# Sink attention and an erf-softplus feed-forward layer: another order of the vector engine's early work and of the early loads

## The chip, the cores and the metric

The kernel runs on one core of a Trainium2 chip. The metric is the device time of one execution in microseconds (us); lower is better. A core has a tensor engine (PE; PEld is its loading of stationary operands), a vector engine (DVE), a scalar engine (ACT), a GpSimd engine (POOL), and a sync engine (SP), which here issues nearly all transfers. Each engine has a queue of instructions that is fixed when the kernel is built.

## The reference

Attention over 4 batches, 8 heads, 768 positions and a head size of 64, with a causal window of 128 positions and 4 "sink" positions that every row sees; its output, as 3072 rows of 512, goes through a feed-forward layer with the gate `h * erf(softplus(h))`. All weights are given in 8-byte floating point.

```python
scores = q @ k.T / sqrt(D)
keep = (pos[None, :] < n_sink) | ((rel >= 0) & (rel < window))
a = softmax(where(keep, scores, -1e9))
x = concat_heads(a @ v)                 # 3072 x 512
h = x @ w_in                            # 512 x 2048
g = h * erf(log1p(exp(h)))
out = g @ w_out                         # 2048 x 512
```

## The kernel before

**Attention.** The rows are worked in 12 groups of 256. A group has four *steps*, one for each pair of heads, so there are steps 0 to 47; steps 0 to 3 are group 0, 4 to 7 group 1, 8 to 11 group 2. A step goes through `prep` (transposes of q and k on PE, copy to `kq` on ACT), `score` (products `ps` on PE; two masked copies L358 and four fused row maxima L363 on DVE, the *maxima* of the step below; four exponentials L367 on ACT), `norm` (sum and reciprocal L374/L375 on DVE, then four multiplications, L380 on ACT for steps 2 to 7; the sink columns `snk` L386 on DVE), `ptrans` (transposes `tp`, `ts` on PE, copies `pa`, `pz` on ACT, selections on POOL), `av` (products on PE) and `xfin` (copies L466 or L471/L472 into the input of the feed-forward layer).

**Feed-forward.** A group has 16 tiles of 128 hidden units. Two of them share one PSUM tile `h`; there are two such tiles in turn, so the pair after next can start only when DVE has read the earlier one. ACT makes `r` and three `u` from a tile (L658 to L663), DVE three products `gf` from them (L667), of which the first also reads `h`. The projection `o` (L687) of a pair needs its third `gf`. Group 0 multiplies in plain f32 with blocks `wf` (L641); from group 1 on `h` uses split blocks `wt` and inputs `xh`, `xl` in three products (L645).

**Weights.** The 32 blocks of 128x512 (16 of `w_in`, 16 of `w_out`) are loaded as 512 KB of 8-byte numbers (`ws`, L531) and turned into f32 blocks `wf` on DVE by three integer instructions each (L543, L548, L551; *conversion* below), in the order of their use (number `wn`). The conversion of block `wn` waits for that of `wn - 2`.

**Order.** Every helper is called with a priority, and a scheduler decides from these, and from its own model of the times, in which order each engine's queue is written. On the chip an engine then takes its queue in that order. `follow(prev, ins)` forces `ins` behind `prev` on an engine and costs no semaphore; `mark` keeps instructions for it: `("t", s)` the last maximum of step s, `("s", s)` its sink columns, `("c", wn)` the end of a conversion, `("p", s)` the last transpose. Eight transfers are in flight at most: each waits for the landing of the one eight places before it.

Of the kernel before, what the change touches and what calls it, by code (L numbers as in the profile page):

```python
# [19 lines left out]
P = 128  # L20
# [20 lines left out]

NM, NA = 2, 8

PW, EA = 256, 12
# [8 lines left out]
def kernel(  # L53
# [77 lines left out]
    def fast_path():  # L131
        with ExitStack() as st:
# [65 lines left out]
            def load(s, what="qk"):  # L198
                g, c = divmod(s, NPAIR)
                b, gb = divmod(g, GPB)  # L200
                d = stp.setdefault(s, {})
                for nm, src in zip("qkv", (q, k, v)):
                    if nm not in what:
                        continue
                    n0 = 1 if nm == "v" else 0
                    t = d[nm] = raw.tile([P, 2 + n0, 2, D], F32, tag=nm, bufs=1 + AL if nm == "v" else 1, name=f"{nm}_{s}")
                    m0 = 0 if gb == 0 else n0
                    for h in range(2):
                        nc.sync.dma_start(
                            t[:, n0 - m0 :, h, :],  # L210
                            src[b, 2 * c + h, gb * GT - m0 * P : (gb + 1) * GT, :].rearrange("(n p) d -> p n d", p=P),
                        )
                if gb == 0 and "v" in what:
                    for z in range(2):
                        for i in range(2):
                            for h in range(2):
                                r0, e = HP * (1 - z) + 2 * SW * i + SW * h, 2 * c + h
                                nc.sync.dma_start(vz[r0 : r0 + SW, z, i, e], v[b, e, :SW, :])
# [92 lines left out]
            def score(s, prev):  # L311
# [37 lines left out]
                for hf, x, y in ((lo, X[0], X[0] + KB), (hi, X[0] + 64, X[0] - 80)):  # L349
                    for t in (both,) if both is not None else ps:  # L350
                        t = t if both is not None else t.rearrange("p (h t) -> p h t", h=1)
                        n = t.shape[1]
                        o, w = (
                            t[hf, :, z : z + 2 * dx].rearrange("p h (i t) -> p h i t", i=2)[:, :, i0:, e : e + 64]
                            for z, e in ((min(x, 64), x - min(x, 64)), (min(y, 64), y - min(y, 64)))
                        )
                        mk = tri[hf].rearrange("p (a b t) -> p a b t", a=1, b=1).broadcast_to([64, n, 2 - i0, 64])
                        nc.vector.copy_predicated(o, mk, w)  # L358
                for i in range(2):
# [11 lines left out]
            def norm(s):  # L371
# [4 lines left out]
                for i in range(2):  # L376
                    for h in range(2):
                        p = pst[:, s % RING, i, h, :P]
                        if NM <= s < NA:
                            nc.scalar.mul(p, p, sm[:, i, h : h + 1])  # L380
                        else:
                            nc.vector.tensor_scalar_mul(p, p, sm[:, i, h : h + 1])
# [8 lines left out]
            def ptrans(s):  # L391
# [4 lines left out]
                for i in range(2):  # L396
                    for h in range(2):
                        mark["p", s] = nc.tensor.transpose(out=tp[:, h, i, :], in_=pst[:, s % RING, i, h, :P], identity=ident)
                nc.tensor.transpose(out=ts, in_=d["snk"], identity=ident)
                pa = d["pa"] = work.tile([P, 2, 2, P], F32, tag="pa", bufs=AL, name=f"pa_{s}")  # L400
# [5 lines left out]
                for hf in (lo, hi):  # L406
                    other = hi if hf == lo else lo
                    y = ts[hf, other].rearrange("p (a b t) -> p a b t", a=1, b=1)
                    nc.scalar.copy(pz[hf, :, :, other], y.broadcast_to([HP, 2, 2, HP]))
                if i0:  # L410
# [97 lines left out]
            def attn(a):  # L508

                for what, fn, s in sorted(plan.get(a, ()), key=lambda x: (STAGES.index(x[0]), x[2])):  # L510
                    with at(a, what):
                        fn(s)
# [11 lines left out]
            def wload(n):  # L524
# [3 lines left out]
                if src.dtype == F32:  # L528
                    nc.sync.dma_start(t[:, :DM].bitcast(F32), src)
                else:  # L530
                    nc.sync.dma_start(t, src.bitcast(I32))  # L531

            def wconv(n, wn):
# [11 lines left out]
                )  # L545
                follow(mark["s", 2] if wn < 1 else mark["t", 3] if wn < 3 else mark["s", 3], first)
                follow(mark.get(("c", wn - 2)), first)
# [39 lines left out]
            for m in range(-LEAD, NG * NF + LAG + 2):  # L587
# [20 lines left out]
                if live:  # L608
                    if f == 0:
                        with at(a, "hid"):  # L610
                            mlp.hidden(hp, xp[g], f)
                    if f % 2 == 1:
                        with at(a, "act"):
                            gs[m // 2] = mlp.act(hp, m, g < 2)

                while wn < 32 and a >= 1 and (wn < (0, 0, 3, 5)[a - 1] if a < 5 else wn < 2 * a - 4 or need(order[wn]) <= m + W1):
                    with at(a, "wc"):
# [10 lines left out]
    class make_mlp:  # L628
# [6 lines left out]

        def hidden(self, hp, xt, f):
            j, fs = f // 4, slice(f % 4 * P, f % 4 * P + P)
            o = hp[:, f % 2, :]
            if len(xt) == 1:
                for c in range(NC):  # L640
                    nc.tensor.matmul(o, wf[NC * j + c][:, fs], xt[0][:, c, :], start=(c == 0), stop=(c == NC - 1))  # L641
                return
# [202 lines left out]
```

## Time and profile before

| | us |
|---|---|
| median of 3 runs | 738.61 (738.1 to 738.76) |
| the profiled execution's own time | 738.85 |
| its span in the trace | 737.1 |
| PE busy | 715.7 (97%) |
| ACT busy | 552.3 (75%) |
| DVE busy | 485.2 (66%) |
| POOL busy | 210.3 (29%) |

Shares are means over the whole span. The change concerns the first 105 us, in which the engines are loaded otherwise than in the rest: there the transfers of the weights, the conversions on DVE and the start of the feed-forward layer lie on top of each other. "Idle before" in a row is the time for which the engine stood still ahead of an instruction, with what ended it.

### The profile page before, as it was taken

The page shows a single profiled execution, that of the slowest core. Times are in us where ns is not written, and L with a number is a line of the kernel's source. Part 1 is how long each engine was busy: PE and PEld are TensorE (multiplying, and loading weights), DVE is VectorE, ACT ScalarE, POOL GpSimd, SP SyncE. Part 2 cuts the span into 40 slices and gives each one's busy share as a digit, 9 for nine tenths or more (in the row PEclk, how much of TensorE's full clock was granted, in tenths as well). Part 3 has the DMA queues.
Part 4 walks back from the last instruction along what each step waited for, and adds up shares of the span by engine and source line. Part 5 has one row for each costly group of instructions (what it writes and reads, how often), then busy time and mean ns, then how long its engine had stood idle before and what let it go on. Part 6 is the DMA issues. An engine that isn't in the chain of part 4 may idle for free. (4 is left out here: it accounts for less than half of the span.)

```text
span 737.1 us, 16408 instructions
## 1 busy us (share of the span) xinstructions
PE 715.7 (97%) x5808; PEld 595.4 (81%) x5808; DVE 485.2 (66%) x1367; ACT 552.3 (75%) x1313; POOL 210.3 (29%) x302
## 2 busy tenths in 40 slices
PE   6789999999999999999999999999999999999997
PEld 3656667766888888888888888888898888898885
DVE  7999997676755665665656666665665566475252
ACT  4687759986877876976975975976886886677572
POOL 3411232111323322332333232233224223233221
PEclk9999999999999999999999999999999999999999
DMA  7999111121222222212212211311321221200000
GB/s 174 278 335 380 31 37 55 31 56 38 76 58 52 51 53 49 65 43 57 67 39 56 76 38 44 83 36 40 78 49 37 79 55 38 67 13 2 29 1 34
DMA packets 113001, 53.07 MB, mean 72 GB/s; under 512 B 91728, under 2 KB 105552, under 8 KB 112912
## 3 DMA queue, kind: packets, MB, share of 16 engines
q1 hardware_dynamic: 112352, 51.87, 26.3%
q8 instruction: 49, 0.80, 0.5%
q14 instruction: 40, 0.33, 0.2%
q10 hardware_dynamic: 560, 0.07, 0.1%
HBM read 38.01 MB, written 6.29 MB: 60 GB/s over the span
## 5 line engine op out<-in xcount | busy, mean ns | idle before, releaser
L645 PE MATMUL h<-xh,wt 128*128 128x256 f32 x1408 | 277.6, 285 | 0.2 <-DVE u L667 0.2
L645 PEld LDWEIGHTS h<-xh,wt 128*128 128x128 f32 x1408 | 223.9, 188 | 7.7 <-issue 1.7
L675 POOL TENSOR_TENSOR g<-u,g 128x512 fp32r<-128x512 f32 x80 | 106.2, 1328 | 341.6 <-DVE g L674 341.0
L645 PE MATMUL h<-xl,wt 128*128 128x256 f32 x704 | 197.9, 282 | 0.0
L663 ACT ACTIVATE u<-r 128x512 f32<-128x512 f32 x288 | 161.7, 622 | 12.6 <-DVE gf L667 4.7
L645 PEld LDWEIGHTS h<-xl,wt 128*128 128x128 f32 x704 | 132.2, 188 | 4.9 <-issue 1.2
L667 DVE SCALAR_TENSOR_TENSOR u<-u,u 128x512 f32<-128x512 f32 x160 | 124.6, 779 | 16.2 <-ACT u L663 1.6
L691 PE MATMUL o<-wt,g 128*128 128x512 f32 x320 | 127.4, 398 | 0.0
L690 PE MATMUL o<-wt,g 128*128 128x512 f32 x320 | 127.3, 398 | 0.0
L692 PE MATMUL o<-wt,g 128*128 128x512 f32 x320 | 123.7, 398 | 0.2 <-POOLq L813 0.2
L667 DVE SCALAR_TENSOR_TENSOR u<-u,h 128x512 f32<-128x512 f32 x80 | 54.9, 687 | 85.8 <-ACT u L663 81.7
L416 POOL TENSOR_SCALAR_AFFINE_SELECT pz<-pa 64x256 f32<-64x256 f32 (+1 forms) x96 | 54.8, 571 | 151.8 <-ACT pa L405 148.5
L367 ACT ACTIVATE pst<-pst,neg 128x144 f32<-128x144 f32 x192 | 77.4, 406 | 27.0 <-DVE neg L363 26.0
L658 ACT ACTIVATE r<-h 128x512 f32<-128x512 f32 x96 | 56.6, 590 | 18.8 <-PE h L645 15.3
L690 PEld LDWEIGHTS o<-wt,g 128*128 128x128 f32 x320 | 60.0, 187 | 11.5 <-ACT ot L696 0.4
L692 PEld LDWEIGHTS o<-wt,g 128*128 128x128 f32 x320 | 59.0, 187 | 12.6 <-POOLq L813 0.7
L691 PEld LDWEIGHTS o<-wt,g 128*128 128x128 f32 x320 | 60.0, 188 | 10.5
L674 DVE CAST g<-u 128x512 fp32r<-128x512 f32 x80 | 34.6, 433 | 45.6 <-PE o L692 42.4
L659 ACT ACTIVATE r<-r 128x512 f32<-128x512 f32 x96 | 60.7, 632 | 2.5
L660 ACT ACTIVATE r<-r 128x512 f32<-128x512 f32 x96 | 60.6, 631 | 2.6
L687 PE MATMUL o<-wf,gf 128*128 128x512 f32 x128 | 58.4, 594 | 1.2 <-DVE gf L667 1.2
L297 ACT COPY kq<-tqk 128x512 f32<-128x512 f32 x48 | 27.8, 581 | 32.5 <-PE tqk L294 30.2
(88 smaller groups left out, 937.3 us busy)
## 6 DMA issues: line engine op xcount, KB each, us to landing
ws<-in_moe_w_in_dram SPq DMA_DIRECT2D x16, 512.0 KB, 6.3
ws<-in_moe_w_out_dram SPq DMA_DIRECT2D x16, 512.0 KB, 8.4
out_dram<-ot SPq DMA_DIRECT2D x24, 256.0 KB, 2.1
v<-in_v_dram SPq DMA_DIRECT2D x56, 96.0 KB, 2.2
q<-in_q_dram SPq DMA_DIRECT2D x80, 64.0 KB, 2.2
k<-in_k_dram SPq DMA_DIRECT2D x80, 64.0 KB, 2.1
vz<-v SPq DMA_DIRECT2D x80, 64.0 KB, 2.0
kq<-kq SPq DMA_DIRECT2D x28, 64.0 KB, 2.0
```

The source lines that it names most:

```text
L367: nc.scalar.activation(y, y, AF.Exp, bias=d["neg"][:, i, h : h + 1], scale=-1.0, accum_out=d["sum"][:, i, h : h + 1])
L645: last = nc.tensor.matmul(o, wt[NC * j + c][:, p, fs], xt[e][:, c, :], start=(m == 0), stop=(m == len(ops) - 1))
L658: nc.scalar.activation(r, h, AF.Tanh, bias=b_t, scale=0.5)
L659: nc.scalar.activation(r, r, AF.Square, bias=b_v, scale=-0.5)
L660: nc.scalar.activation(r, r, AF.Square, bias=b_r)
L663: sq = nc.scalar.activation(u, r, AF.Square, bias=b_a[i], scale=CS)
L667: pr = nc.vector.scalar_tensor_tensor(out=acc, in0=u, scalar=CC[i] * CS**2, in1=x, op0=ALU.add, op1=ALU.mult)
L675: nc.gpsimd.tensor_tensor(gl, acc, gh.bitcast(F32), op=ALU.subtract)
L687: nc.tensor.matmul(o, gt[0][:, ws], wf[16 + f], start=(f == 0), stop=(f == NF - 1))
L690: behind(nc.tensor.matmul(o, gh[:, ws], wt[16 + f][:, 0, :], start=(f == 0), stop=False))
L691: nc.tensor.matmul(o, gh[:, ws], wt[16 + f][:, 1, :], start=False, stop=False)
L692: nc.tensor.matmul(o, gl[:, ws], wt[16 + f][:, 0, :], start=False, stop=(f == NF - 1))
```

## The change

1. The conversion of block 0 follows the maxima of step 1 (before: the sink columns of step 2), may be scheduled from the first pass on, and the maxima of step 2 are put behind it.
2. The loads of q, k and v of group 2 are put behind the last weight load on SP.
3. The first instruction of the conversions 8, 10, 13 and 17 gets a fixed place: behind the maxima of step 4, the sink columns of step 4, the maxima of step 5, the sink columns of step 5.
4. Four smaller rules: the maxima of step 3 follow the sink columns of step 1; the multiplications of step 3 follow the `pz` copy of step 2; the first feed-forward product follows the `ts` transpose of step 2; `norm` of step 3 is called later in its pass.

No instruction is added or removed; places in the queues change.

```diff
+TURN = {8: ("t", 4), 10: ("s", 4), 13: ("t", 5), 17: ("s", 5)}
...
-                        nc.sync.dma_start(
-                            t[:, n0 - m0 :, h, :],
-                            src[b, 2 * c + h, gb * GT - m0 * P : (gb + 1) * GT, :].rearrange("(n p) d -> p n d", p=P),
-                        )
+                        x = src[b, 2 * c + h, gb * GT - m0 * P : (gb + 1) * GT, :].rearrange("(n p) d -> p n d", p=P)
+                        follow(mark["w"] if g == 2 else None, nc.sync.dma_start(t[:, n0 - m0 :, h, :], x))
...
-                        nc.vector.copy_predicated(o, mk, w)
+                        follow(mark["c", 0] if s == 2 else mark["s", 1] if s == 3 else None, nc.vector.copy_predicated(o, mk, w))
...
-                            nc.scalar.mul(p, p, sm[:, i, h : h + 1])
+                            follow(mark["pz", 2] if s == 3 else None, nc.scalar.mul(p, p, sm[:, i, h : h + 1]))
...
-                for what, fn, s in sorted(plan.get(a, ()), key=lambda x: (STAGES.index(x[0]), x[2])):
+                for what, fn, s in sorted(plan.get(a, ()), key=lambda x: (STAGES.index(x[0]) + 1.5 * (x[::2] == ("norm", 3)), x[2])):
...
-                follow(mark["s", 2] if wn < 1 else mark["t", 3] if wn < 3 else mark["s", 3], first)
+                follow(mark["t", 1] if wn < 1 else mark["t", 3] if wn < 3 else mark["s", 3], first)
+                follow(mark[TURN[wn]] if wn in TURN else None, first)
                 follow(mark.get(("c", wn - 2)), first)
...
-                            mlp.hidden(hp, xp[g], f)
+                            mlp.hidden(hp, xp[g], f, lambda ins: follow(mark["ts", 2], ins))
...
-                while wn < 32 and a >= 1 and (wn < (0, 0, 3, 5)[a - 1] if a < 5 else wn < 2 * a - 4 or need(order[wn]) <= m + W1):
+                while wn < 32 and a >= 1 and (wn < (1, 1, 3, 5)[a - 1] if a < 5 else wn < 2 * a - 4 or need(order[wn]) <= m + W1):
```

Where this puts instructions is seen in the queues. On DVE, behind the last maximum of step 1 (`neg_245`), before; `ps_1_299` and `ps_0_298` are the scores of step 2:

```order
L363 ISA pst,neg_245<-ps_0_246,mask_79 128x144
L363 ISA neg_245 128x1
L358 COPY_PREDICATED ps_1_299<-tri,ps_1_299 64x64
L358 COPY_PREDICATED ps_0_298<-tri,ps_0_298 64x64
...
L363 ISA pst,neg_297<-ps_1_299,mask_80 128x144
```

and in the change, at the same place (`ws_143` is block 0; the scores of step 2 have new numbers):

```order
L364 ISA pst,neg_245<-ps_0_246,mask_79 128x144
L364 ISA neg_245 128x1
L544 TENSOR_SCALAR wf_268<-ws_143 128x512
L550 SCALAR_TENSOR_TENSOR wf_268<-ws_143,wf_268 128x512
L553 SCALAR_TENSOR_TENSOR wf_268<-ws_143,wf_268 128x512
L359 COPY_PREDICATED ps_0_306<-tri,ps_0_306 64x64
L359 COPY_PREDICATED ps_1_307<-tri,ps_1_307 64x64
```

The three instructions of block 0 have come from behind the scores of step 3 to ahead of those of step 2.

On DVE around step 4 (`ps_539`), before; `ws_174`, `ws_176` and `ws_178` are the blocks 5 to 7:

```order
L548 SCALAR_TENSOR_TENSOR wf_467<-ws_174,wf_467 128x512
L358 COPY_PREDICATED ps_539<-tri,ps_539 64x2x2x64
L548 SCALAR_TENSOR_TENSOR wf_558<-ws_176,wf_558 128x512
L551 SCALAR_TENSOR_TENSOR wf_467<-ws_174,wf_467 128x512
L543 TENSOR_SCALAR wf_558<-ws_178 128x512
L358 COPY_PREDICATED ps_539<-tri,ps_539 64x2x2x64
L551 SCALAR_TENSOR_TENSOR wf_558<-ws_176,wf_558 128x512
L548 SCALAR_TENSOR_TENSOR wf_558<-ws_178,wf_558 128x512
L363 ISA pst,neg_538<-ps_539,mask 128x144
```

and in the change; `ws_272` is block 9, whose load stands right behind that of block 8 (`ws_183`) on SP:

```order
L550 SCALAR_TENSOR_TENSOR wf_467<-ws_174,wf_467 128x512
L550 SCALAR_TENSOR_TENSOR wf_558<-ws_176,wf_558 128x512
L553 SCALAR_TENSOR_TENSOR wf_467<-ws_174,wf_467 128x512
L544 TENSOR_SCALAR wf_558<-ws_178 128x512
L553 SCALAR_TENSOR_TENSOR wf_558<-ws_176,wf_558 128x512
L550 SCALAR_TENSOR_TENSOR wf_558<-ws_178,wf_558 128x512
L553 SCALAR_TENSOR_TENSOR wf_558<-ws_178,wf_558 128x512
L544 TENSOR_SCALAR wf_579<-ws_272 128x512
L359 COPY_PREDICATED ps_539<-tri,ps_539 64x2x2x64
L550 SCALAR_TENSOR_TENSOR wf_579<-ws_272,wf_579 128x512
L359 COPY_PREDICATED ps_539<-tri,ps_539 64x2x2x64
L553 SCALAR_TENSOR_TENSOR wf_579<-ws_272,wf_579 128x512
```

The copies and maxima of step 4 have moved behind the end of block 7 and behind the first instruction of block 9; block 8, which rule 3 holds behind the maxima, is now converted after block 9 has begun.

On PE at the start of group 1's feed-forward, before, behind seven products of the first pair `h_1252`; `h_1333` is the second pair, which takes over the PSUM tile of group 0's last pair, and `av_1052` and `ps_1077` are steps 7 and 8:

```order
L453 MATMUL av_1052<-pz_948,vz 64x64 x8
L345 MATMUL ps_1077<-kq 64x208 x2
L345 MATMUL ps_1077<-kq 64x224 x2
...
L294 MATMUL tqk_1137<-ident,k_1102 128x128 x2
L294 MATMUL tqk_1137<-ident,q_1099 128x128 x2
L645 MATMUL h_1252<-xl_743,wt_1186 128x256
L645 MATMUL h_1252<-xh_742,wt_1186 128x256
L645 MATMUL h_1333<-xh_742,wt_1121 128x256
L645 MATMUL h_1333<-xl_743,wt_1121 128x256
```

and in the change, behind the six products of `h_1252` with the first two blocks:

```order
L649 MATMUL h_1252<-xh_742,wt_1145 128x256
L649 MATMUL h_1333<-xh_742,wt_1121 128x256
L649 MATMUL h_1333<-xl_743,wt_1121 128x256
...
L691 MATMUL o_0_852<-wf_996,gf_1173 128x512
L691 MATMUL o_1_853<-wf_996,gf_1173 128x512
...
L649 MATMUL h_1252<-xh_742,wt_1186 128x256
L649 MATMUL h_1333<-xh_742,wt_1186 128x256
L454 MATMUL av_1052<-pa_947,v_early_149 64x64 x2
```

`av_1052`, `ps_1077`, `tqk_1137` and the three products of `h_1252` with the third block stood ahead of `h_1333` and stand behind it now.

## Rows read from the trace of the kernel before

**Rows 1.** Windows by stage: busy us (x instructions) of each engine, granted clock, DMA share, GB/s.
```profile
20.00:25.00 5.00, 2.74 (x36) 1.71 (x36) 4.91 (x18) 4.59 (x17) 2.52 (x5) 1.00 1.11 278
25.00:30.00 5.00, 5.00 (x37) 4.39 (x38) 5.00 (x12) 4.03 (x12) 2.75 (x6) 0.66 1.02 302
...
50.00:80.00 30.00, 29.27 (x167) 18.21 (x168) 29.75 (x79) 22.31 (x60) 3.30 (x6) 1.00 0.86 311
80.00:100.00 20.00, 18.98 (x139) 13.10 (x134) 20.00 (x38) 14.85 (x31) 11.46 (x7) 1.00 0.12 27
100.00:120.00 20.00, 19.91 (x137) 14.24 (x134) 17.01 (x52) 14.07 (x38) 2.61 (x4) 1.00 0.08 21
```

**Rows 2.** Timeline of PE: start, us, line, out<-in, count [idle before <-releaser].
```profile
79.40 0.67 PE L453 MATMUL av<-pa,v_early 128*64 128x64 f32 x12 [0.73 <-ACT pa L405]
...
82.94 2.43 PE L641 MATMUL h<-xf,wf 128*128 128x256 f32 x10 [0.92 <-DVE wf L551]
```

**Rows 3.** Timeline of DVE between the maxima of steps 1 and 2.
```profile
14.38 0.08 DVE L363 DVE_READ_ACCUMULATOR2_ANT neg<- 128x1 f32 x1
16.55 0.62 DVE L358 COPY_PREDICATED ps<-tri,ps 64x64 f32<-64x64 int8 x3 [2.09 <-PE ps L345]
```

**Rows 4.** Timeline of SP's issues; then landings of those same issues (KB, us).
```profile
4.41 0.47 SPq L531 DMA_DIRECT2D ws<-in_moe_w_in_dram  x1
...
23.67 1.53 SPq L531 DMA_DIRECT2D ws<-in_moe_w_in_dram  x1
...
29.18 3.46 SPq L531 DMA_DIRECT2D ws<-in_moe_w_out_dram  x1
...
36.99 1.42 SPq L531 DMA_DIRECT2D ws<-in_moe_w_out_dram  x3
...
ws<-in_moe_w_in_dram SPq DMA_DIRECT2D x1, 512.0 KB, 4.4
...
ws<-in_moe_w_in_dram SPq DMA_DIRECT2D x1, 512.0 KB, 6.2
...
ws<-in_moe_w_out_dram SPq DMA_DIRECT2D x1, 512.0 KB, 6.9
...
ws<-in_moe_w_out_dram SPq DMA_DIRECT2D x1, 512.0 KB, 3.9
```

**Rows 5.** Timeline of DVE from block 5 to block 9.
```profile
30.11 0.41 DVE L543 TENSOR_SCALAR wf<-ws 128x512 int32<-128x512 int32 x1
...
32.29 0.42 DVE L358 COPY_PREDICATED ps<-tri,ps 64x256 f32<-64x256 int8 x1
...
36.29 0.31 DVE L363 CUSTOM_DVE_ANT_0 pst<-ps,mask 128x144 f32<-128x144 f32 x1
...
37.21 0.42 DVE L543 TENSOR_SCALAR wf<-ws 128x512 int32<-128x512 int32 x1
37.54 0.68 DVE L551 SCALAR_TENSOR_TENSOR wf<-ws,wf 128x512 int32<-128x512 int32 x1
38.15 0.68 DVE L548 SCALAR_TENSOR_TENSOR wf<-ws,wf 128x512 int32<-128x512 int32 x1
...
39.24 0.17 DVE L374 TENSOR_SCALAR sum<-sum 128x4 f32<-128x4 f32 x1 [0.41 <-ACT pst L367]
...
40.89 0.43 DVE L543 TENSOR_SCALAR wf<-ws 128x512 int32<-128x512 int32 x1 [0.81 <-DMA ws<-in_moe_w_out_dram]
```

**Rows 6.** Timeline of PE at the start of group 1's feed-forward.
```profile
98.82 0.86 PE L453 MATMUL av<-pa,v_early 128*64 128x64 f32 x12
...
101.41 0.36 PE L645 MATMUL h<-xl,wt 128*128 128x256 f32 x1
101.61 0.59 PE L645 MATMUL h<-xh,wt 128*128 128x256 f32 x2
```

**Rows 7.** Timeline of DVE at the same place.
```profile
100.13 0.41 DVE L472 TENSOR_TENSOR xl<-av,xh 128x256 fp32r<-128x256 f32 x1
...
101.08 0.69 DVE L667 SCALAR_TENSOR_TENSOR gf<-u,h 128x512 f32<-128x512 f32 x1
```

More of the change, by code (lines that the diff above doesn't have):

```diff
@@ L398, in ptrans @@
                         mark["p", s] = nc.tensor.transpose(out=tp[:, h, i, :], in_=pst[:, s % RING, i, h, :P], identity=ident)
-                nc.tensor.transpose(out=ts, in_=d["snk"], identity=ident)
+                mark["ts", s] = nc.tensor.transpose(out=ts, in_=d["snk"], identity=ident)
                 pa = d["pa"] = work.tile([P, 2, 2, P], F32, tag="pa", bufs=AL, name=f"pa_{s}")
@@ L408, in ptrans @@
                     y = ts[hf, other].rearrange("p (a b t) -> p a b t", a=1, b=1)
-                    nc.scalar.copy(pz[hf, :, :, other], y.broadcast_to([HP, 2, 2, HP]))
+                    mark["pz", s] = nc.scalar.copy(pz[hf, :, :, other], y.broadcast_to([HP, 2, 2, HP]))
                 if i0:
@@ L528, in wload @@
                 if src.dtype == F32:
-                    nc.sync.dma_start(t[:, :DM].bitcast(F32), src)
+                    mark["w"] = nc.sync.dma_start(t[:, :DM].bitcast(F32), src)
                 else:
-                    nc.sync.dma_start(t, src.bitcast(I32))
+                    mark["w"] = nc.sync.dma_start(t, src.bitcast(I32))
             def wconv(n, wn):
@@ L634, in hid_tile, with hidden @@
             return self.ps_h.tile([P, 2, GT], F32, tag="h", name=f"h_{m}")
-        def hidden(self, hp, xt, f):
+        def hidden(self, hp, xt, f, first=lambda ins: ins):
             j, fs = f // 4, slice(f % 4 * P, f % 4 * P + P)
@@ L640, in hidden @@
                 for c in range(NC):
-                    nc.tensor.matmul(o, wf[NC * j + c][:, fs], xt[0][:, c, :], start=(c == 0), stop=(c == NC - 1))
+                    x = nc.tensor.matmul(o, wf[NC * j + c][:, fs], xt[0][:, c, :], start=(c == 0), stop=(c == NC - 1))
+                    if f == c == 0:
+                        first(x)
                 return
```

## The prediction

> **What bounds the kernel now.** Read the windows by stage first [rows 1]. From 50 us on the tensor engine is busy for 29.27 of 30 us, then 18.98 of 20, then 19.91 of 20: its work is fixed, so the kernel ends later by whatever more it stands idle, and earlier by what idleness goes away. Second, see who it stands waiting for. The same windows give the vector engine 29.75 of 30 us and 20.00 of 20 up to 100 us, and only 17.01 of 20 behind that. Both engines are full up to 100 us, and the tensor engine alone after it. The two waits of the tensor engine in this stretch are 0.73 us at 79.40 and 0.92 us at 82.94, the second for the last conversion instruction L551 of a weight block [rows 2]. A third, smaller one carries no mark: at 101.61 two products take 0.59 us, of which the second is the first of the pair h_1333 [rows 6]; its PSUM tile comes free when the vector engine's first product with the last pair of group 0 ends, at 101.08 + 0.69 = 101.77 [rows 7]. So up to 101.8 us the vector queue paces the tensor queue. That is the account to keep: how much earlier or later does the vector queue reach these two places, and where does the tensor queue stand then?
>
> **The change part by part.**
>
> *Block 0 into the gap.* The vector engine stands idle for 2.09 us, from 14.46 to 16.55, until the scores of step 2 are there [rows 3]. The block was issued at 4.41 and landed 4.4 us later, at 8.8 [rows 4]. Chained, its three instructions last 0.42 + 0.68 + 0.68 = 1.78 us [rows 5], up to 16.24: step 2 does not get later, and 0.3 us of idleness is left. Later the queue is shorter by three starts, 0.33 + 0.61 + 0.61 = 1.55 us (37.21 to 37.54 to 38.15) [rows 5]. Taken alone: a gain of 1.55 us on the vector engine.
>
> *Where that gain goes.* Block 5 is issued at 23.67 and lands 6.2 us later, at 29.87 [rows 4]; before, the vector engine asked for it at 30.11 [rows 5]. Coming 1.55 us earlier it asks at 28.56 and waits for 1.3 us. The loads up to here are issued as before, so the block lands no earlier. Block 6 cannot be issued before 23.67 + 1.53 = 25.20 [rows 4], and with the same 6.2 us it lands at 31.4. From there on the lead is nothing, give or take 0.3 us: what is late next is the transfer.
>
> *Block 9 ahead of step 4's maxima.* Before, between block 6 and 37.54 the vector engine did two masked copies of 0.42 us (one shown), four maxima (36.29 to 37.21, 0.92 us) and the first instruction of block 8 (0.33): 2.1 us in all [rows 5]. In the change these stand behind the first instruction of block 9. The queue therefore comes to that instruction at 37.54 - 2.1 + 0.61 = 36.05, with block 7 ended. When does block 9 land? Its load is issued behind block 8's, whose issue ends at 29.18 + 3.46 = 32.64 and whose data land at 29.18 + 6.9 = 36.08 [rows 4]. From below: 32.64 + 3.9 (the landing of an issue at 36.99 into a queue that was running dry) = 36.5. From above: 32.64 + 6.9, as long as block 8 itself, = 39.5. I take the time behind block 8: 512 KB at the 311 GB/s of the full stage 50 to 80 [rows 1] are 1.7 us, and weight blocks alone go somewhat faster, so about 1.4 us: 37.5. The vector engine waits for 1.4 us there. Behind it stand the copies and maxima of step 4; for the maxima wait the exponentials on the scalar engine, and behind those its first r of the feed-forward layer. The maxima come to 37.5 + 0.33 + 0.42 + 0.61 + 0.42 + 0.61 = 39.9 instead of 36.29, so the first projection is at most 3.6 us later. The size does not matter to the end: the waits at 79.40 and 82.94 take up 1.65 us of it, and the last term below the remaining 1.95.
>
> *The sum on the vector engine.* At 37.5 the changed queue has 2.1 us of work open that was done before, and 0.61 us done that was open: 1.5 us behind. Before, the vector engine then waited 0.41 us for exponentials and 0.81 us for block 9 [rows 5]. In the change the blocks from 10 on follow each other on the bus ahead of their turns, and the exponentials have more conversions ahead of their sums, so these 1.2 us go. Left: 0.2 us later, with ends of -0.8 (block 9 at 36.5) and +2.2 (at 39.5).
>
> *Group 2's loads, and the small rules.* The ten loads wait behind the last weight. Group 2's transposes, which need them, have their turn on the tensor engine behind 82.94, and in 80 to 100 the transfer engines are busy for a share of 0.12 only [rows 1]: no cost, and a landing of some 4 us [rows 4] if that cover were gone. What they give is the earlier blocks 9 and up, counted above. The fixed turns of blocks 10, 13 and 17 and the rules on step 3 set an order in a queue that is full anyway: nothing, give or take 0.3 us.
>
> *The pair h_1333.* Here is the term that decides. Before, the tensor queue had the rest of step 7's and step 8's work (av_1052, ps_1077, tqk_1137) and the products of h_1252 with the third block ahead of h_1333. From 98.82 to 101.77 [rows 6, 7] that was 2.9 us of work while the vector engine came to the instruction that frees the tile. In the change this work stands behind h_1333 and behind the projection that follows it. The tensor engine comes to the pair at the same 98.8 (its content up to there is the same, and the vector queue paces it at 82.94 as before, plus 0.2). The vector engine frees the tile at 101.77 + 0.2, less 0.3 because one xl (0.41, with overlap some 0.3) now stands behind it: 101.7. The tensor engine stands for 2.9 us, and then still has those 2.9 us of work to do. Behind it nothing gives this back, since in 100 to 120 it was idle for 0.09 us in all [rows 1]. Later by 2.9 + 0.2 - 0.3 = 2.8 us.
>
> [...] Could queues pass a wait, the order would not matter and the sum would be the 0.2 us of the vector account. The trace agrees as far as it can: the second product at 101.61 held all behind it until 101.77 [rows 6, 7].
>
> *Sum.* 738.85 us for the profiled execution, plus 2.8, is 741.65. The median of the runs lies 0.24 us under it: **741.4 us**. With the vector account's ends: 740.4 to 743.4.
>
> **The rivals.**
>
> *The loads are there when asked for (not slower).* If blocks 5 and 9 land before the vector engine asks, at 28.56 and about 34.5, no wait is left: its account is 1.55 + 1.2 = 2.75 us better. Then the tile is free at 101.77 - 0.3 - 2.75 = 98.7, just when the tensor engine came there before, and the end moves by 2.9 - 0.3 - 2.75 = -0.15 us: 738.5. If only block 9 is early, 1.2 us better: 740.0. The point that decides is block 5's landing, 29.87 now. For it speaks that fewer loads stand in the queue, against it that those in front of block 5 are unchanged.
>
> *The vector queue is ahead by more than the loads explain (faster).* The tensor engine would have to come through without the 0.73 and 0.92 us and without the wait at h_1333: -1.65 us, 737.0. That takes the freed tile by 97.2 rather than 101.7, 4.5 us. Nothing in the rows gives more than 2.75; but a full vector queue can hide waits of instructions for each other, and the changed order interleaves other pairs.
>
> *The clock falls in a new pause (still slower).* [...] Two pauses are new: one before the first projection, where later waits take the loss up, and 2.9 us at h_1333, where nothing does: 741.4 + 1.7 = 743.1. [...] Against it: in 80 to 100 the clock stayed at 1.00 through a wait of 0.92 us.
>
> **How the numbers follow.** The forecast has 0.48 (740.4 to 742.8); the clock rival and a late block 9 have 0.12 (742.8 to 744); the early loads 0.25 (738.4 to 740.0); the faster rival 0.15 (about 737). A measurement tells 0.2% (1.48 us, below 737.1 or above 740.1) from no change. So slower 0.60, same 0.25, faster 0.15. The range leaves out most of the faster rival and the upper end of the clock rival: 737.6 to 743.1. The forecast's own range is 740.4 to 742.8.
>
> **What would show it.** Right: the vector engine's wait at 14.46 shrinks to 0.3 us; new waits for a weight load of 1.3 us near 28.6 and 1.4 us near 36.1, the second ended by a load of w_out; the maxima of step 4 near 39.9; the wait at 79.40 gone; a wait of 2 to 3 us of the tensor engine near 99, ended by the vector engine's gf; tensor idle time over the span up by about 2.8 us. Wrong: if block 9 lands before 36 us, or if the vector engine's first product with group 0's last pair ends before 99 us, the sum fails at that term; if all these waits are there and the end is not later, the tensor engine had slack behind 102 us that I did not see.

## The result, and the profile after

The change makes the kernel slower: 743.71 us (median of 5 runs, 742.08 to 746.21), against 738.76 (738.1 to 739.45) for the kernel before beside it. The ratio is 1.0072, with an interval of 1.0058 to 1.0087. That is 4.95 us by the medians and 5.3 by the ratio, where 2.8 were forecast. The direction and the place were right; the size was outside the range.

The profiled execution of the change took 746.21 us, the longest of its five, with a span of 744.5. Its rows must not be read as if they were those of the median. So the same kernel was run and profiled once more (*again* below): median 743.16 of 6 runs, profiled execution 743.71, span 741.9. Both are shown, and where they differ, that is what two executions of one program differ by.

First the windows of the changed kernel, in the columns of [rows 1]. Compare the granted clock, behind the five busy times.

```profile
20.00:25.00 5.00, 1.39 (x8) 0.78 (x7) 4.88 (x20) 3.97 (x14) 1.79 (x4) 0.94 1.17 304
25.00:30.00 5.00, 4.65 (x34) 3.56 (x35) 4.43 (x11) 4.07 (x14) 3.00 (x7) 0.50 0.92 255
...
50.00:80.00 30.00, 30.00 (x158) 19.82 (x158) 29.69 (x72) 23.17 (x56) 5.66 (x10) 0.97 0.88 294
80.00:100.00 20.00, 19.48 (x119) 12.57 (x118) 19.97 (x46) 15.73 (x38) 4.49 (x6) 1.00 0.03 7
100.00:105.00 5.00, 3.09 (x17) 2.64 (x16) 5.00 (x9) 2.97 (x6) 1.13 (x2) 0.79 0.36 79
105.00:110.00 5.00, 5.00 (x36) 2.64 (x36) 3.08 (x6) 0.00 (x0) 0.00 (x0) 0.87 0.01 3
100.00:120.00 20.00, 18.09 (x136) 12.91 (x135) 14.11 (x42) 9.62 (x24) 1.13 (x2) 0.91 0.15 34
```

From 20 to 50 us the tensor engine was busy for 22.09 of 30 us, before for 24.27: this is the lateness that the prediction has later waits take up. From 50 to 100 us it stood idle for less than before: 30.00 of 30 and 19.48 of 20. The new idle time is in 100 to 120, where it was busy for 19.91 before [rows 1] and is now for 18.09. And a second loss doesn't show as idle time: from 100 to 110 the granted clock is 0.79 and 0.87 (0.50 in 103 to 106, 1.00 from 106.5 on), so (0.21 + 0.13) x 5 = 1.7 us of full clock are missing while PE counts as busy.

The timeline of PE of the changed kernel, columns as in [rows 2]:

```profile
53.70 3.60 PE L691 MATMUL o<-wf,gf 128*128 128x512 f32 x8
...
84.11 7.17 PE L643 MATMUL h<-xf,wf 128*128 128x256 f32 x32 [0.52 <-DVE gf L671]
...
102.98 0.58 PE L649 MATMUL h<-xh,wt 128*128 128x256 f32 x1 [1.91 <-DVE gf L671]
...
104.43 4.52 PE L691 MATMUL o<-wf,gf 128*128 128x512 f32 x8
...
124.57 1.99 PE L691 MATMUL o<-wf,gf 128*128 128x512 f32 x4 [0.44 <-ACT ot L700]
...
178.66 0.89 PE L399 MATMUL tp<-ident,pst 128*128 128x128 f32 x4 [0.88 <-DVE pst L383]
...
188.01 0.55 PE L454 MATMUL av<-pa,v 128*64 128x128 f32 x8 [0.73 <-ACT pz L412]
```

The wait at 79.40 of [rows 2] is gone. At 102.98 stands the pair h_1333, 1.91 us late, ended by the vector engine's `gf` as forecast. The eight projections at 104.43 take 4.52 us where eight of the same form at 53.70 took 3.60: this is how the low clock looks in a timeline. Two waits follow that [rows 1] had no room for, 0.44 us for an output copy and 0.88 us for multiplications of the vector engine. The last row is an instruction that can be found in every kernel here. In the timeline of the kernel before it is this one:

```profile
180.86 0.55 PE L453 MATMUL av<-pa,v 128*64 128x128 f32 x8 [0.73 <-ACT pz L411]
```

From it to the end of the span are 737.1 - 180.86 = 556.2 us before and 744.5 - 188.01 = 556.5 after. So 7.15 of the 7.4 us that this execution lost lie ahead of that row.

The timeline of DVE of the changed kernel, at the places that the vector account spoke of:

```profile
11.58 1.66 DVE L383 TENSOR_SCALAR pst<-pst,sum 128x128 f32<-128x128 f32 x4
...
17.08 0.76 DVE L359 COPY_PREDICATED ps<-tri,ps 64x64 f32<-64x64 int8 x4
...
29.91 0.43 DVE L544 TENSOR_SCALAR wf<-ws 128x512 int32<-128x512 int32 x1 [0.43 <-DMA ws<-in_moe_w_in_dram]
...
32.88 0.43 DVE L544 TENSOR_SCALAR wf<-ws 128x512 int32<-128x512 int32 x1 [1.94 <-DMA ws<-in_moe_w_in_dram]
...
38.65 0.43 DVE L544 TENSOR_SCALAR wf<-ws 128x512 int32<-128x512 int32 x1 [0.89 <-DMA ws<-in_moe_w_out_dram]
...
41.35 0.31 DVE L364 CUSTOM_DVE_ANT_0 pst<-ps,mask 128x144 f32<-128x144 f32 x1
...
102.25 0.67 DVE L671 SCALAR_TENSOR_TENSOR gf<-u,h 128x512 f32<-128x512 f32 x1
```

Blocks 5, 6 and 9 are waited for, 3.26 us in sum, and the maxima of step 4 come at 41.35 instead of 36.29 [rows 5]. The product that frees the tile starts at 102.25, before at 101.08 [rows 7].

### The profile page after: what moved, and what is told of

It is laid out like the page before. It is cut to its first block, busy times and chain, and to the rows that moved or that the text cites. A ratio compares the mean times of both kernels' runs of the same rounds, so it can differ in the third digit from the quotient of the medians.

```text
span 744.5 us, 16415 instructions
## 1 busy us (share of the span) xinstructions
PE 719.1 (97%) x5808; PEld 597.9 (80%) x5808; DVE 488.4 (66%) x1367; ACT 553.5 (74%) x1313; POOL 203.0 (27%) x302
## 5 line engine op out<-in xcount | busy, mean ns | idle before, releaser
L417 POOL TENSOR_SCALAR_AFFINE_SELECT pz<-pa 64x256 f32<-64x256 f32 (+1 forms) x96 | 48.3, 503 | 163.9 <-ACT pa L406 160.6
```

## The experiments

Medians and ratios are to the kernel before, run on the same chip beside each (738.64 to 739.0 us). The diffs show the lines that decide; lines that only keep an instruction for `follow` are left out. An edit fixes the order at its place only: behind it the scheduler writes the queues otherwise as well. In the kernel with fourteen products of 3, in 4, 5 and the second of 7, PE's order differs in places up to between 145 and 180 us, so what they show is sure for the pair and less so for what comes after it.

**1. The changed kernel once more** (no edit).

> The changed kernel once more, for a second trace. If what the first trace shows belongs to the order of the queues, the same waits come back: the vector engine's waits for block 6 and block 9 near 33 and 38, the tensor engine's wait ahead of h_1333 of 1.5 to 2.9 us near 102, and a median of 743.7 +- 1. If the first trace was an odd execution (746.21, the slowest of its five), the wait ahead of h_1333 is there but the granted clock behind it is 1.00, and the execution takes 742 to 744.

Measured: 743.16 us, ratio 1.0065 [1.0051, 1.0078]. Its timelines of DVE:

```profile
16.66 0.76 DVE L359 COPY_PREDICATED ps<-tri,ps 64x64 f32<-64x64 int8 x4 [0.37 <-PE ps L346]
...
29.38 0.43 DVE L544 TENSOR_SCALAR wf<-ws 128x512 int32<-128x512 int32 x1 [0.32 <-DMA ws<-in_moe_w_in_dram]
...
30.70 0.43 DVE L544 TENSOR_SCALAR wf<-ws 128x512 int32<-128x512 int32 x1 [0.29 <-DMA ws<-in_moe_w_in_dram]
...
36.69 0.43 DVE L544 TENSOR_SCALAR wf<-ws 128x512 int32<-128x512 int32 x1 [1.19 <-DMA ws<-in_moe_w_out_dram]
...
39.39 0.31 DVE L364 CUSTOM_DVE_ANT_0 pst<-ps,mask 128x144 f32<-128x144 f32 x1
...
100.27 0.68 DVE L671 SCALAR_TENSOR_TENSOR gf<-u,h 128x512 f32<-128x512 f32 x1
```

and of PE:

```profile
82.12 7.17 PE L643 MATMUL h<-xf,wf 128*128 128x256 f32 x32 [0.41 <-DVE gf L671]
...
101.00 0.57 PE L649 MATMUL h<-xh,wt 128*128 128x256 f32 x1 [1.93 <-DVE gf L671]
...
122.67 1.98 PE L691 MATMUL o<-wf,gf 128*128 128x512 f32 x4 [0.45 <-ACT ot L700]
...
176.08 0.89 PE L399 MATMUL tp<-ident,pst 128*128 128x128 f32 x4 [0.29 <-DVE pst L383]
...
185.43 0.55 PE L454 MATMUL av<-pa,v 128*64 128x128 f32 x8 [0.73 <-ACT pz L412]
```

The loads differ between two executions of one program (block 6 was waited for 1.94 us there, 0.29 here), and the vector account with them: the tile is free at 102.98 in the one, 101.00 in the other, 101.77 before. Yet the pause is 1.91 and 1.93 us. That is so because both engines start from one common wait: 84.11 to 102.98 are 18.87 us, 82.12 to 101.00 are 18.88. Before, from 82.94 (there a conversion is waited for [rows 2]) to 101.77 [rows 7], they were 18.83. The order between two common waits fixes the pause; a late load moves both ends. Where no wait is marked there (82.83, in the kernel with the loads not moved of experiment 8), the pause is 1.41 us.

**2. The loads of blocks 8 and 9 exchanged** in the changed kernel.

```diff
-... + [(wload, n) for n in order[8:W0]]
+... + [(wload, order[9])]
...
-                            wload(n)
+                            wload(order[8] if n == order[9] else n)
```

> The changed kernel with the loads of blocks 8 and 9 exchanged; all other queues are the same. Theory (block 9 ahead of step 4's maxima holds the vector queue): the vector engine's wait for block 9, 0.89 us, is gone, step 4's maxima stand at 40.4 instead of 41.35, the tile of h_1333 is free up to 0.9 us earlier, and the end is 0 to 0.9 us earlier: 742.8 to 743.7. Rival (block 6's landing and the start of step 2 are what matter, and block 8's lateness takes the place of block 9's): 743.7.

Measured: 743.91 us, 1.0060 [1.0046, 1.0073]. The wait for block 9 is gone, and one for block 8 stands in its place (timeline of DVE, then of PE):

```profile
39.87 0.43 DVE L544 TENSOR_SCALAR wf<-ws 128x512 int32<-128x512 int32 x1 [0.83 <-DMA ws<-in_moe_w_out_dram]
```

```profile
81.36 7.17 PE L643 MATMUL h<-xf,wf 128*128 128x256 f32 x32 [0.24 <-DVE gf L671]
...
100.24 0.39 PE L649 MATMUL h<-xh,wt 128*128 128x256 f32 x1 [1.93 <-DVE gf L671]
```

The pair starts 0.76 us earlier than in *again*, and the pause is 1.93 us again (18.88 us behind the common wait). The end is not earlier. The wait for block 9 is thus not where the time is lost.

**3. Zero products in the pause.** Products with a zero operand, which add nothing to `h`, behind the sixth product of `h_1252`, just ahead of `h_1333`: seven in one kernel, fourteen in the other.

```diff
+                if m == 5 and self.zero is not None:
+                    for _ in range(7):
+                        self.warm = last = nc.tensor.matmul(o[:, :P], wt[NC * j][:, 0, fs], self.zero, start=False, stop=False)
+                    self.zero = None
...
-                            ahead = mlp.hidden(hp, xp[g], f)
+                            ahead = mlp.hidden(hp, xp[g], f, lambda ins: follow(mlp.warm if m == 18 else None, ins))
```

> The changed kernel with 7 products with zeros in the pause ahead of h_1333 (0.8 us of 1.93); all queues are otherwise word for word those of the changed kernel. Theory (the pause brings the clock down, and 1.1 us of it is too short for that, as the 1.20 us ahead of the first projection of the kernel before was): a remaining wait of 1.1 us, granted clock 1.00 from 100 to 110, 1.7 us less than the 743.2 to 743.7 of the changed kernel: 741.5 to 742.0. Rival (what the fuller filling gained came from the order that moved with it, not from the clock): 743.2 to 743.7.

> The changed kernel with 14 products with zeros of 128 columns put into the pause ahead of h_1333 (about 1.6 us, as long as the transposes of 128 columns take); they add nothing to the output. The wait itself stays, filled with empty work. Theory (the pause brings the clock down): the granted clock behind it stays at 1.00, the eight projections take 3.6 us instead of 4.5, and the end is earlier by up to 1.7 us: 742.0. Rival (the clock falls whatever the tensor engine does there, or the fall costs nothing): 743.7.

Measured with seven: 743.32 us, 1.0062 [1.0049, 1.0075]. Apart from the seven, and GpSimd's setting of the zeros at the start, all queues are as in the change. The timeline of PE:

```profile
101.35 0.38 PE L652 MATMUL h<-xh,wt 128*128 128x256 f32 x1 [0.54 <-DVE gf L680]
...
102.16 3.60 PE L700 MATMUL o<-wf,gf 128*128 128x512 f32 x8
...
121.38 1.98 PE L700 MATMUL o<-wf,gf 128*128 128x512 f32 x4 [0.45 <-ACT ot L709]
...
188.23 0.41 PE L295 MATMUL tqk<-ident,k 128*128 128x128 f32 x2 [0.30 <-ACT ot L709]
...
196.07 0.50 PE L703 MATMUL o<-wt,g 128*128 128x512 f32 x1 [0.50 <-DVE g L687]
...
197.62 0.69 PE L399 MATMUL tp<-ident,pst 128*128 128x128 f32 x3 [0.24 <-DVE pst L383]
```

The clock stayed at 1.00, and the eight projections take 3.60 us. From the pair to the wait for the output copy are 20.03 us, against 21.59 in the change and 21.67 in *again*: here is what the low clock costs, 1.6 us. But the gain does not reach the end. Behind 188 us the engine stands in three new waits, 1.04 us together, and the median is that of the change within its interval. With fourteen: 740.52 us (11 runs), 1.0025 [1.0016, 1.0034]; the pair no longer waits at 101.55. This kernel is 2.6 to 3.2 us better than the change, but PE's order differs in places from 102 to 174 us too, and the vector engine's from 132 us on, so how much of it is the clock's is not shown.

**4. The pair behind the transposes again**, alone, in the changed kernel: `h_1333` follows `tqk_1137`, as it did before.

```diff
-                            ahead = mlp.hidden(hp, xp[g], f)
+                            ahead = mlp.hidden(hp, xp[g], f, lambda ins: follow(mark["q", 9] if m == 18 else None, ins))
```

> The changed kernel with the pair h_1333 put behind the transposes tqk_1137 again; the vector queue is the same up to the instruction that frees the pair's tile. Theory (the pair's place decides): 2.9 us of other work covers the wait of 1.91 us, and if no pause means no low clock, a further 1.7 us: 740.1 to 741.8. Rival (the vector engine's lateness sets the end wherever the pair stands): the wait only moves, 743.7.

Measured: 740.83 us, 1.0033 [1.0020, 1.0046]. The timeline of PE:

```profile
101.24 5.33 PE L693 MATMUL o<-wf,gf 128*128 128x512 f32 x8 [2.50 <-DVE gf L673]
```

One line gives back 2.3 us (against *again*) to 2.9 us (against the first runs of the change), and the intervals do not meet. This is the place. In the profiled execution the next projection now waits instead, for 2.50 us, and the clock is 0.66 in 100 to 105. That execution took 742.32 us, while three of the five took 740.5 to 740.8, so its row need not be that of the median.

**5. The early pair alone, in the kernel before**: `av_1052` and `ps_1077` are put behind the sixth product of `h_1333`; no other rule is changed.

```diff
+                            ahead = mlp.hidden(hp, xp[g], f, lambda ins: [follow(ins, y) for x, y in mark.items() if x[:2] in (("av", 7), ("ps", 8))] if m == 18 else None)
```

> The kernel before with one difference: step 7's products av_1052 and step 8's scores ps_1077 are put behind the sixth product of h_1333. The vector queue is the same up to the product that frees the pair's tile. Theory (the pair's place decides, and a pause of 2 us and more brings the clock down): a pause of 2.7 us near 99 until 101.8, granted clock 0.66 in the 5 us behind it, and an end later by 2.6 + 1.7 = 4.3 us: 742.9. Rival (the pause alone, the clock stays): 741.3. Rival (the order does not matter): 738.6.

Measured: 745.37 us, 1.0091 [1.0077, 1.0105]. Timeline of PE and one window:

```profile
100.29 0.47 PE L645 MATMUL h<-xl,wt 128*128 128x256 f32 x1 [1.92 <-DVE xl L472]
...
101.49 0.58 PE L645 MATMUL h<-xh,wt 128*128 128x256 f32 x1 [0.52 <-DVE gf L669]
```

```profile
100.00:105.00 5.00, 4.19 (x40) 3.56 (x40) 4.44 (x8) 1.59 (x3) 0.00 (x0) 0.55 0.01 3
```

The early pair alone is enough for a loss of 6.6 us, without block 0, the loads or the turns. That is 2.3 us more than the theory had. Its account up to the `av` row (187.65, so 6.8 us later): waits of 2.44 us, clock (0.45 + 0.23) x 5 = 3.4 us (0.77 was granted in 105 to 110), and 0.84 us of a wait at 178.30: 6.7 us. It closes less well than it looks: this execution came out of the wait for L551 at 82.26, so 0.68 us earlier than before, and of the 7.5 us lost from there on some 0.8 are in none of these terms.

**6. All of the old order around the pair, in the changed kernel**: as in 4, and also the projection, the input split of step 6 and `u` and `gf` around it.

```diff
+                        mlp.project(gs[w // 2], g2, f2, lambda ins: follow(mark["q", 9] if w == 12 else ahead if live and f and g >= 2 else None, ins))
...
+                            gs[m // 2] = mlp.act(hp, m, g < 2, {
+                                ("u", 1): mark["xh", 6], ("u", 2): mark["k", 8], ("g", 0): mark["xl", 6]} if m == 15 else {}, follow)
```

> The changed kernel with the tensor queue, and with it the copies that feed it (xh and xl of step 6, kq of step 8), in the order of the kernel before around h_1333: av_1052, ps_1077 and tqk_1137 ahead of the pair and of the next projections. Theory: 2.9 us of work covers the pause, no wait over 1 us is left near 100, the granted clock from 100 to 110 is 1.00, and the end is earlier by 1.9 + 1.7 + 0.4 (a wait for the output copy) = 4.0 us than the 743.2 to 743.7 of the changed kernel: 739.2 to 739.7. Rival (the vector engine's lateness shows up in the next product that waits for it, as it did behind the pair alone): 740.8 as there, with a low clock.

Measured: 745.26 us, 1.0099 [1.0082, 1.0116]; no gain. The timeline of PE says why it doesn't isolate what it was to isolate:

```profile
103.09 0.39 PE L650 MATMUL h<-xl,wt 128*128 128x256 f32 x1 [1.58 <-DVE xl L473]
...
171.65 1.09 PE L399 MATMUL tp<-ident,pst 128*128 128x128 f32 x4 [3.26 <-DVE pst L383]
```

The pause is still there, now for `xl`, and a new wait of 3.26 us comes 70 us later. Orders forced on three engines at one place shift what the scheduler writes behind it. The edit was too wide to speak for or against the theory.

**7. The group-2 loads alone, and with the pair put behind** (both on the kernel before; the second has the line of experiment 4 too).

```diff
+                        x = src[b, 2 * c + h, gb * GT - m0 * P : (gb + 1) * GT, :].rearrange("(n p) d -> p n d", p=P)
+                        follow(mark["w"] if g == 2 else None, nc.sync.dma_start(t[:, n0 - m0 :, h, :], x))
```

> The kernel before with part 2 of the change alone: group 2's loads behind all weights. This also moves h_1333 ahead of av_1052 in the tensor queue, and blocks 9 and up may land earlier. Theory (the pair's place decides, whichever part brings it): the vector engine's wait for block 9 of 0.81 us near 40 goes, a pause of 1.5 to 2.9 us stands near 99, and the end is 2 to 4.3 us later: 740.6 to 742.9. Rival (the cost lies in block 0's place and the order around step 4): 737.8 to 738.6.

> The kernel before with part 2 alone (group 2's loads behind all weights) and with h_1333 held behind tqk_1137. Theory: the vector engine frees the pair's tile at 99.8 as with part 2 alone, the tensor engine has 2.9 us of other work by then, so the 0.89 us of wait is gone, and the end is 0.9 us earlier than the 739.2 with part 2 alone: 738.3, or 0.4 us ahead of the kernel before. Rival (the wait moves to the next product that needs the vector engine, as it did behind the pair in the changed kernel): 739.2.

Measured, loads alone: 739.16 us (11 runs), 1.0015 [1.0005, 1.0026]. The timeline of PE:

```profile
99.79 0.38 PE L643 MATMUL h<-xh,wt 128*128 128x256 f32 x1 [0.89 <-DVE gf L665]
```

The loads alone also bring the pair forward, yet cost little, 0.4 us by the medians and 1.1 by the ratio (a time that neither the theory nor the rival had): the vector engine is 2 us ahead there (the tile is free at 99.79 instead of 101.77), so 0.89 us of pause is left, and the clock stays at 1.00. Holding the pair back in this kernel makes it worse, 743.31 us, 1.0070 [1.0053, 1.0086]; what waits then is step 7's product (timeline of PE), with a clock of 0.66 in 100 to 105:

```profile
100.83 1.12 PE L451 MATMUL av<-pa,v_early 128*64 128x64 f32 x12 [1.53 <-ACT kq L295]
```

So "late pair" is no remedy by itself: the end is 4 us later than with the loads alone, where the theory had it 0.9 us earlier and the rival the same. Why `kq` comes late there was not asked. That the early pair costs little when the engine that must free its tile is ahead fits the loads alone; no run isolates it.

**8. Block 0 alone on the kernel before, the change without block 0, and the change without the loads' move.** The first has part 1's lines alone, the second takes them back, the third is

```diff
-                        follow(mark["w"] if g == 2 else None, nc.sync.dma_start(t[:, n0 - m0 :, h, :], x))
+                        follow(None, nc.sync.dma_start(t[:, n0 - m0 :, h, :], x))
```

> The kernel before with part 1 of the change alone: block 0 between the maxima of steps 1 and 2. The vector queue then has the first instructions of blocks 8, 9 and 10 ahead of step 4's maxima (part 3 is what holds block 8 back), and h_1333 ahead of av_1052. Theory (the vector queue waits in order for each load): the maxima of step 4 not before the landing of block 10, 42 us or later, the first projection 4 us or more later than 49.7, and a pause near 99 as well: 742 to 746. Rival (the 1.55 us won on the vector engine reach the end): 737.1.

> The changed kernel without part 1: block 0 behind the sink columns of step 2 again, the other parts kept. Block 9 then stands behind the maxima of step 4, and h_1333 behind av_1052, ps_1077 and tqk_1137. Theory (part 1 brings block 9 ahead of step 4's maxima and the pair ahead of its cover): the first projection near 48.7 to 49.7, no wait of 1.9 us near 100, granted clock 1.00 from 100 to 110: 738.0 to 739.5. Rival (the parts 2 to 4 carry a cost of their own): 741 or more.

> The changed kernel without part 2: group 2's loads where they were, among the blocks 9 to 14; the tensor queue around h_1333 is the same. Theory (the pause at h_1333 is counted from the wait before it, so the size of the vector engine's lateness moves all that follows): block 9 lands 2 us or more later, the maxima of step 4 and the first projection move by as much, and the end is 1 to 3 us later: 744.5 to 746.5. Rival (group 2's loads are hidden and the lateness is taken up before 100 us): 743.2 to 743.7.

Block 0 alone: 751.05 us, 1.0161 [1.0147, 1.0175]. The timelines of DVE and PE:

```profile
36.77 0.43 DVE L543 TENSOR_SCALAR wf<-ws 128x512 int32<-128x512 int32 x1 [2.02 <-DMA ws<-in_moe_w_out_dram]
```

```profile
46.90 1.77 PE L345 MATMUL ps<-kq 64*64 64x208 f32 x16 [5.90 <-DVE neg L363]
```

Without the other parts the vector engine stands still for 2.02 us before a load of `w_out`, step 4's maxima come at 45.75, and PE stands for 5.90 us: a loss of another kind and at another place. The change without block 0: 738.90 us (11 runs), 1.0001 [0.9992, 1.0009]. Maxima at 35.65, no wait of more than 1 us near 100 us, clock 1.00. So parts 2 to 4 cost nothing without part 1, and the loss comes with part 1, by way of the queues that the scheduler then writes. The change without the loads' move: 745.07 us, 1.0080 [1.0063, 1.0096], not to be told from the change. The time lies in the theory's range, but its mechanism is not there: in the profiled execution block 9 was waited for until 36.99, against 36.69 in *again*, where 2 us and more were forecast.

## Why the forecast had the right sign and the wrong size

Five kernels have the same PE queue (seven zero products apart, and one transpose near 60 us in the kernel with the loads not moved). Their rows say where the time goes. The first column is the start of `h_1333`; behind the clock stand the starts of the wait for `ot`, of the `av` row and of the next `ts` transpose behind that (in the kernel before at 193.41):

| kernel | pair | clock 100 to 105 | 105 to 110 | `ot` row | `av` row | `ts` row | span |
|---|---|---|---|---|---|---|---|
| the change | 102.98 | 0.79 | 0.87 | 124.57 | 188.01 | 200.66 | 744.5 |
| again | 101.00 | 0.66 | 1.00 | 122.67 | 185.43 | 198.32 | 741.9 |
| blocks 8, 9 exchanged | 100.24 | 0.66 | 1.00 | 121.95 | 184.80 | 198.72 | 742.4 |
| loads not moved | 101.19 | 1.00 | 1.00 | 121.23 | 183.97 | 198.49 | 742.0 |
| seven zero products | 101.35 | 1.00 | 1.00 | 121.38 | 184.22 | 198.21 | 741.7 |

From the pair to the `ot` row are 21.59, 21.67 and 21.71 us with the low stretch and 20.04 and 20.03 without. The way to the `av` row of before (180.86) can then be added up. *Again*: tile free 0.77 us earlier than before, +2.9 of work that now stands behind the pair, +1.6 of clock, +0.45 and +0.29 of new waits: 4.47, measured 4.57. The profiled execution of the change: +1.21 + 2.9 + 1.6 + 0.44 + 0.88 = 7.03, measured 7.15. Seven zero products: -0.42 + 2.9 + 0.73 = 3.2, measured 3.36.

Behind the `av` row the lead of the last three kernels goes. From the `ts` row to the end there are 543.5 to 543.8 us in all five and in the kernel before, so all is settled by 201 us. Between the two rows PE stands still in these three kernels ahead of the transposes of the next k, until 188.97, 188.60 and 188.23 us. Blocks 8 and 9 exchanged, timeline of PE:

```profile
188.97 0.41 PE L295 MATMUL tqk<-ident,k 128*128 128x128 f32 x2 [0.46 <-DMA k<-in_k_dram]
```

Here the profile names the load of k; in the other two it names the scalar engine (0.86 us with the loads not moved, 0.30 with seven zero products). In the change and in *again* PE has no such wait there; why is not shown. Waits for `g` and `tp` up to 198 us, as in experiment 3, take the rest of the lead.

- **Block 0 in the gap: right.** Idle time left 0.37 us in *again* (0.3 forecast); step 2's copies 0.1 us later there, 0.5 in the other execution.
- **Waits for blocks: right in kind.** Forecast 1.3 + 1.4 us (blocks 5, 9). Measured 0.43 + 1.94 + 0.89 and 0.32 + 0.29 + 1.19: block 6 was forecast at none, and its wait is what differs most. Maxima of step 4 forecast at 39.9, measured 41.35 and 39.39.
- **Vector account: right within its ends.** Tile free at 101.7 by the forecast (101.8 with its own figures, 1.49 - 1.22 being 0.27 and not 0.2), with ends 1.0 earlier and 2.0 later; measured 102.98 in the change's execution and 101.00 in *again*.
- **Group 2's loads: no cost, as forecast, or a small one.** Alone they give 0.4 to 1.1 us; without them the change is not faster.
- **The pause: 2.9 forecast, 1.9 measured, and no matter to the sum.** Before, PE had done six of these 32 products (80.46, 1.56 us) when it came to the wait at 82.94, and 26 were left; now all 32 stand behind the wait (84.11), so PE comes later to `h_1333` than the 98.8 that the forecast kept. But the sum goes by when the tile is free and by how much work stands behind it, and these 2.9 us were right: the accounts close with them to 0.2 us. The sum took it that neither queue passes an instruction that waits; the traces have PE standing still for 1.91 us (the change) and 1.93 us (*again*) ahead of `h_1333`, with `av_1052`, `ps_1077` and `tqk_1137` behind it.
- **The step that failed: what stands behind the pair was put at nothing.** The sum ended with the pause, and the low clock was put aside as a rival of 0.12 with one row against it, that the clock stayed at 1.00 through 0.92 us; the pause that the same text forecast was three times as long. What the runs show in its place is 2.3 to 3.9 us lost there in every one of the five executions (lateness of the `ts` row, less that of the pair, less 2.9). In three of them 1.6 us of it are the low clock, the size priced (1.7); with that the sum would be 741.4 + 1.6 = 743.0. The 1.7 are (1 - 0.66) x 5 us, an estimate from the granted clock in 25 to 30 of [rows 1]; that a pause at the pair brings the clock down was assumed, and in 100 to 110 three of the five executions miss 1.7 us of full clock and two miss none. But the two at full clock lost 2.8 and 2.3 us there as well, in waits. So the clock is shown as a cost up to the `ot` row, and not as what parts the median from the forecast.
- **The waits behind it.** Up to the `av` row they are 0.74 us (*again*), for `ot` and `tp`. "Behind it nothing gives this back" was read from 0.09 us of idle time in 100 to 120; what else a late stretch might meet was not asked. That lateness makes these waits isn't shown: from 101 to 176 us the change's PE queue also has projections and steps in another order than before, and no run tells the two apart.
- **The sign by idle time: misjudged.** PE's idle time over the span was to rise by about 2.8 us. It rose by 4.0 in the change's execution and by 1.2 in *again*, whose span rose by 4.8: part of the loss counts as busy.

What is shown: that the early pair is enough for a loss of this kind (experiment 5), that without part 1 there is none (8), that holding the pair back in the change returns 2.3 to 2.9 us (4), and what the low clock costs up to the `ot` row. What stays open: whether the end would be earlier without the low clock. From the `av` row to the end there are 556.2 us before, 556.5 in the change and in *again*, but 557.5 to 558.0 in the other three, so a kernel that came earlier lost some of it again before its `ts` row, and the medians of all five lie within 743.2 to 745.1. Why block 6 lands 2.2 us later in one execution than in the other (32.88 against 30.70, both waits ended by it) isn't shown either.

Near 100 us the clock was low (0.55 to 0.79 granted in 100 to 105) behind waits of 1.91, 1.92, 1.93, 1.93 and 2.50 us, and at 1.00 behind 0.54 and 0.89. The length alone doesn't settle it: low (0.66) behind 1.53 (experiment 7), 1.00 behind 1.41 (loads not moved), 1.58 (experiment 6) and, at 45.16 in the change without block 0, 1.94. What else it goes by is not shown.

## What to carry to other kernels

When two queues of fixed order meet at a shared buffer, write down what stands between two waits that both engines go through: work that moved from ahead of a wait to behind it counted whole in the accounts here (2.9 us), though not one instruction is new. If the same sum forecasts a pause of the tensor engine longer than any that the profile of before shows with a full clock, give the lower clock a real weight in the range: here it came in three of five executions of one queue (0.66 to 0.79 granted in 100 to 105). Ask as well what the late stretch meets further on: here 2.3 to 3.9 us were lost there, with the low clock and without. And look at two profiled executions before explaining a difference in waits for loads: here one program showed 0.29 and 1.94 us for the same block.

## What the runs showed of the hardware that was not expected

The low clock did not show as idle time: with 0.79 and 0.66 granted in 100 to 105, eight projections took 4.52 us (the change) and 4.60 (*again*) instead of 3.60 and count as busy in full.

Four multiplications of the vector engine (L383) took 1.66 us at 11.58 in the change's execution, 0.87 at 11.48 in *again*. In the first a copy on GpSimd ran beside them, from 12.04 to 13.15; in the second it began at 12.27, when they were nearly done. The last of the four began at 12.17, just behind the copy's start, and ended at 12.17 + 1.07 = 13.24, just behind the copy's end at 13.15. No run here took the copy away, so whether it held the multiplication up is not shown.
